# Local x transposed by DMA with its sums later in the block, and quarter products issued one by one

## The chip, the cores and the metric

The kernel runs on one core of one Trainium2 chip. A core has a matrix engine (TensorE, PE in the profile, with its weight loads PEld), VectorE (DVE), ScalarE (ACT), GpSimd (POOL) and SyncE (SP), each with its own in-order instruction queue, and 16 DMA engines that move data between memories. The metric is the device time of one execution in microseconds (us). Before the change the median of three runs is 294.25 us (293.95 to 294.44). The profile is of one execution of 294.54 us, of which the program's instructions span 292.8 us; TensorE's granted clock was 0.999 of full speed.

## The reference

Attention over 8 batches, 8 heads, 576 positions and head size 64, with two fixed masks, followed by a dense layer pair on all 4608 tokens.

```python
scores = scale * np.matmul(q, k.transpose(0, 1, 3, 2))
mask_local = (rel >= 0) & (rel < stride)                     # heads 0 to 3, stride 32
mask_strided = (rel >= 0) & (pos[None, :] % stride == pos[:, None] % stride)   # heads 4 to 7
...
scores = np.where(masks[None, :, :, :], scores, -1000000000.0)
attn = exp(scores - max) / (sum + 1e-09)
x = (attn @ v).transpose(0, 2, 1, 3).reshape(4608, 512)
h = x @ w_in                                                 # 512 -> 2048
g = h * np.tanh(log1p(exp(h)))                               # Mish
out = g @ w_out                                              # 2048 -> 512
```

## The kernel before

**Tiling.** The 4608 tokens are worked in nine blocks of 512 (block t). In block t the kernel runs three things interleaved on the same engines: the first layer of block t (class `Mlp1`), the second layer of block t-1 (class `Mlp2`), and the attention of batch t+1 (class `Attn`, blocks 1 to 6 for batches 2 to 7). Blocks 7 and 8 have no attention left. x, the attention's output, is kept transposed in `xT` (128 x 4 x ring of four batches of 576 tokens): chunks 0 and 1 hold the local heads, chunks 2 and 3 the strided ones.

**Seven products for eight.** Both layers are multiplied as 2 x 2 blocks by a scheme of seven products and extra sums. For the first layer, the sums of weights lie in `wis`, the sums of x in `xs`; they are made by `x_sum` (line 370), called x0 to x3: x0 uses strided x alone, x1, x2 and x3 use local x too. The second layer has sums `gs` of the activations (`g_sum`, line 458: n for the first, then g1, g2, g3). All these sums are `tensor_tensor` operations of DVE with two operands in SBUF.

**First layer, by quarters.** `Mlp1.step` (line 402) works quarter group g (0 to 3) of the 2048 columns in named steps, on three PSUM banks be, al and E of one of two sets. A product is four matmuls of 256 columns (`prod`, line 386). Step a: product 5 into E, its cast to s5, product 1 into al, a copy be<-al. Step b: product 6 on al, its cast to s2, product 3 on E, the sum h0 = E + s2 on DVE, product 2 on be. Step c: product 7 on al, the sum h1 = al + s5 on DVE. Step d: product 4 on al. Steps U, W and H are the Mish activations of be, al and h, on ACT. Casts go to ACT where there is attention (t + 1 < 8), else to DVE; the copy be<-al is always ACT's.

**Second layer.** `Mlp2.steps` (line 539) gives 14 half steps, here m1 to m14, of eight matmuls each, in the order of products 1, 5, 2, 6, 3, 7, 4, each in two halves. After m2, m4 and m8 ACT copies a bank out; after m10 and m12 DVE adds the output sum (`add(Dv, osb...)`, lines 520 and 523) from PSUM and one SBUF operand; after m12 and m14 SP stores 256 rows. m11 and m12 write the bank al (product 7), which m12's output sum reads and which m13 (product 4) writes next.

**Attention.** Step q n computes a group of scores on PE (`qk`, line 261; strided groups 0 to 2, local groups 3 to 5), takes exp on ACT and multiplies by the mask (`mask`, line 283) on POOL; in block 2 groups 0 to 3 are masked on DVE. Steps v take from the list `v_steps` (line 721): five strided PV groups, two strided transposes, and the local part: PV, PV, transposes, PV, PV, transposes. A PV group (`pv`, line 293) is six or seven matmuls into the banks at0 and at1 in turn, a reciprocal and a multiply on DVE. A local transpose (`xt`, line 324) is six PE transposes (line 330) into PSUM and one DVE copy to `xT` (line 334).

**What sets the order.** The program's order is written out by hand: a plan string (MAIN for t = 3 to 6, MAIN2 for t = 2, PLAIN for t = 7 and 8; lines 804 to 819) names the steps in sequence, and `run` (line 712) issues each, so every engine's queue holds its instructions in the plan's order. In a plan, x, g and n are sums on DVE, m a half step of the second layer, q a group of scores, s the copy of v, e and f loads of ACT's tables for exp and Mish, D the four DMA transposes of q and k on SP's queue, R POOL's small copies that wait for them and then its loads of later batches.

Of the kernel before, what the change touches and what calls it, by code (L numbers as in the profile page):

```python
# [45 lines left out]
def kernel(ctx, tc, q, k, v, moe_w_in, moe_w_out, out):  # L46
# [69 lines left out]
    def cast(eng, out_, in_):  # L116
        if eng is Sc:
            Sc.copy(out_, in_)  # L118
        else:
            eng.tensor_copy(out_, in_)  # L120

    def add(eng, out_, a, b, op=ALU.add):
        eng.tensor_tensor(out=out_, in0=a, in1=b, op=op)  # L123
# [114 lines left out]
    class Attn:  # L238
# [54 lines left out]
        def pv(self, kind, n0, n1, bank, eng=None):  # L293
# [27 lines left out]
                in1=rden[0:m, 0:nu].unsqueeze(2).to_broadcast([m, nu, D]), op=ALU.mult,  # L321
            )

        def xt(self, kind, hf, bank, eng):
            tr = bank[:].bitcast(BF16)
            t0 = (self.b % RING) * S
            if kind == "l":
                for w in range(NW):
                    u = 12 * hf + 2 * w
                    PE.transpose(  # L330
                        tr[:, WQ * w:WQ * w + WQ], x_l[0:WQ, u:u + 2, :].rearrange("p u d -> p (u d)"),
                        ident[0:WQ, 0:WQ],
                    )
                cast(eng, xT[:, hf, t0:t0 + S], tr[:, 0:S])
            else:
                for j in range(CS):
                    u = 16 * hf + 2 * j
                    PE.transpose(  # L338
                        tr[:, PN * j:PN * j + PN], x_s[0:PN, u:u + 2, :].rearrange("p u d -> p (u d)"),
                        ident[0:PN, 0:PN],  # L340
                    )
                cast(
                    eng, xT[:, 2 + hf, t0:t0 + S].rearrange("p (n j) -> p n j", j=CS),
                    tr[:, 0:576].rearrange("p (j n) -> p n j", j=CS),
                )
# [35 lines left out]
    class Mlp1:  # L381
# [18 lines left out]
                    )  # L400

        def step(self, s, g):
            z = (self.t + g + 1) % 2
            be, al, E = [x[:] for x in SETS[z]]
            if self.eng is Dv:
                z = ((self.t + 1) % 2, 2, self.t % 2, (self.t + 1) % 2)[g]
                be, al, E = [x[:] for x in ((A1, A0, SETS[(self.t + 1) % 2][2]) if g == 1 else SETS[z])]
            h = hh[z]
            o = gT[:, 4 * g:4 * g + 4, :]
            two = lambda x: x.rearrange("p (u n) -> p u n", u=2)  # L410
            if s == "a":
                self.prod(5, g, E, True)
                cast(self.eng, s5[z][:], E)
                self.prod(1, g, al, True)
                Sc.copy(be, al)  # L415
            elif s == "b":
                self.prod(6, g, al, False)
                cast(self.eng, s2[z][:], al)
                self.prod(3, g, E, False)
                add(Dv, h[:, 0, :], E, s2[z][:])  # L420
                self.prod(2, g, be, False)
            elif s == "c":
                self.prod(7, g, al, False)
                add(Dv, h[:, 1, :], al, s5[z][:])
            elif s == "d":
                self.prod(4, g, al, False)
            elif s == "H":
                Sc.activation(  # L428
                    o[:, :, 256:512], h[:].rearrange("p i (u n) -> p (i u) n", u=2), AF.Mish
                )  # L430
            elif s == "U":
                Sc.activation(o[:, 0:2, 0:256], two(be), AF.Mish)
            elif s == "W":
                Sc.activation(o[:, 2:4, 0:256], two(al), AF.Mish)  # L434
# [130 lines left out]
    with tc.manual_schedule():  # L565
# [146 lines left out]
        def run(plan, t):  # L712
# [8 lines left out]
            def v_steps():  # L721
# [4 lines left out]
                def xt(kind, hf):  # L726
                    at.xt(kind, hf, (A0, A1)[bank[0]], Sc if t == 1 and kind == "l" else Dv)
                    bank[0] = (bank[0] + bank[1]) % 2
                P = lambda kd, r: (lambda: pv(kd, r))
                X = lambda kd, hf: (lambda: xt(kd, hf))  # L730
                if t == 1:
# [3 lines left out]
                    )  # L735
                return (
                    [P("s", r) for r in PV_S] + [X("s", 0), X("s", 1)]
                    + [P("l", r) for r in PV_L[:2]] + [X("l", 0)]
                    + [P("l", r) for r in PV_L[2:]] + [X("l", 1)]
                )  # L740
            vs_ = late + (v_steps() if at else [])
            late.clear()
            JOBS = [("s", 0), ("s", 1), ("s", 2), ("l", 0), ("l", 1), ("l", 2)]
            for w in plan.split():
                c, n = w[0], int(w[1:]) if len(w) > 1 else 0
                if c in "abcdHUW":
                    m1.step(c, n)
                elif c == "p":
                    plain(t, n, deal1[n], act=False)
# [52 lines left out]

        late = []
        MAIN = (
            "x0 m m e m m x1 s x2 g1 g2 q0 q1 m m m m g3 q2 q3 m m q4 q5 m D v m f R a0 v v m m v v b0 a1 x3 c0 v "
            "U0 v b1 d0 U1 W0 c1 v a2 d1 W1 v H0 a3 v v b2 v H1 c2 b3 c3 d2 W2 v H3 d3 n U2 U3 W3 H2"
        )
        SECOND = (
            "t0 p0 q2 p1 t1 t2 t3 w1 p2 q3 w2 p3 q5 q4 p4 h p5 p6 f v y0 D y1 p7 s v p8 R y3 y6 v y2 v p9 v v y5 y4 "
            "p10 p11 y9 p12 y8 y7 y11 v v p13 v y13 p14 y10 p15 y14 n v y12 w3 y15"  # L810
        )
        MAIN2 = (
            "v m m v m e v x0 x1 m x2 g1 q1 q0 g2 m m m m g3 q2 s q3 m m q4 q5 m D f v m v a0 R v m m v v b0 a1 x3 "
            "c0 v v b1 d0 U0 U1 W0 c1 v a2 d1 W1 v H0 a3 v v b2 v c2 H1 b3 c3 d2 W2 v H3 d3 U2 U3 W3 H2 n"
        )
        PLAIN = (
            "m m x0 g1 x1 m m x2 x3 a0 m m g2 m b0 m m m g3 m m c0 U0 a1 H0 m m b1 d0 W0 a2 c1 a3 b2 b3 c3 d1 U2 H1 "
            "W1 U1 c2 d3 W3 U3 d2 H2 W2 H3 n"
        )

        for t in range(1, NBLK):
# [40 lines left out]
```

## Time and profile before

| | us |
|---|---|
| median of three runs (lowest, highest) | 294.25 (293.95, 294.44) |
| the profiled execution | 294.54 |
| its span | 292.8 |
| a block with attention (3 to 6) | 29.59 to 29.68 |
| a plain block | 25.19 to 25.39 |

The profile page lists busy time by engine; a view by windows gives the same for stretches of the span, and the timeline lists instructions in order of time with start, duration, engine, line, operation, output<-inputs, shapes and, in brackets, how long the engine was idle before it and who ended the wait. Durations of pipelined matmuls and activations overlap, so work is read from start to start. POOL's six masks of a block (three of 72 partitions, then three of 128) run back to back; block 4's first five:

| mask | start us | us |
|---|---|---|
| strided 0 | 143.86 | 1.81 |
| strided 1 | 145.64 | 2.79 |
| strided 2 | 148.40 | 1.26 |
| local 0 | 149.63 | 2.00 |
| local 1 | 151.59 | 1.99 |

### The profile page before, as it was taken

Reading aid. Unit: us, or ns where it says so; the run is one execution under the profiler, and the core shown is the slowest. Engines: PE = TensorE matmul, PEld = TensorE weight load, DVE = VectorE, ACT = ScalarE, POOL = GpSimd, SP = SyncE. Lnnn points to the kernel's source line nnn. Section 1 sums busy time; section 2 is a strip of 40 time slices with the busy share of each in tenths; the row PEclk is TensorE's granted clock in tenths of the full one; section 3 lists DMA queues with packets and bytes.
Section 4 is the critical chain, followed back from the end, with each engine's and each line's share of the span. In section 5 each row is a group of like instructions: output and inputs, shape, how many; then the busy total and the mean of one; then the engine's idle time right before and its main releaser. Section 6 shows DMA issues by size and latency. Waiting matters only on the chain.

```text
span 292.8 us, 7799 instructions
## 1 busy us (share of the span) xinstructions
PE 282.4 (96%) x3256; PEld 223.8 (76%) x3268; DVE 205.7 (70%) x387; ACT 204.7 (70%) x361; POOL 102.7 (35%) x109
## 2 busy tenths in 40 slices
PE   8889999999999999999999999999999999999995
PEld 3564545545788888888888888888898888888884
DVE  2583548587798896688768866886688667757842
ACT  2578793769667789778977898789878526825650
POOL 8754330131614533981399039502920000000000
PEclk9999999999999999999999999999999999999999
DMA  7999999999999999999699989950110003003004
GB/s 136 179 204 202 203 194 185 174 169 150 137 154 181 204 174 70 165 223 166 32 167 215 167 39 147 231 36 2 72 73 2 2 29 118 1 3 143 2 0 143
DMA packets 94415, 35.84 MB, mean 122 GB/s; under 512 B 75804, under 2 KB 90124, under 8 KB 94380
## 3 DMA queue, kind: packets, MB, share of 16 engines
q0 software_dynamic: 61712, 18.71, 70.1%
q1 hardware_dynamic: 31708, 15.73, 24.4%
q10 hardware_dynamic: 960, 0.91, 1.0%
q8 instruction: 25, 0.41, 0.6%
q14 instruction: 10, 0.08, 0.1%
HBM read 37.87 MB, written 9.44 MB: 162 GB/s over the span
## 4 chain that ended last, share of the span: by engine, by line
PE 77%; ACT 8%; DVE 7%; issue 3%; DMA 3%; POOL 1%; ACTq 0%; POOLq 0%
PE al L129 34%; PE ee L129 19%; PE be L129 12%; PE at L129 5%; DVE hh L123 4%; PE at L310 3%; ACT s L118 3%; DMA vraw<-in_v_dram 3%; ACT gT L428 1%; PE at L338 1%; ACT Pl L281 1%; ACT gT L434 1%; DVE x_l L319 1%; ACT be L415 1%; PE at L330 1%
## 5 line engine op out<-in xcount | busy, mean ns | idle before, releaser
L129 PEld LDWEIGHTS <-w_in 128*128 128x128 bf16 x464 | 44.3, 98 | 20.6 <-issue 5.0
L129 PEld LDWEIGHTS <-gs 128*128 128x128 bf16 x512 | 48.7, 98 | 6.3 <-DVE gs L123 0.3
L129 PEld LDWEIGHTS <-wis 128*128 128x128 bf16 x472 | 44.5, 99 | 9.2 <-issue 3.2
L129 PEld LDWEIGHTS <-gT 128*128 128x128 bf16 x448 | 42.0, 98 | 10.0
L287 POOL TENSOR_TENSOR Ps<-Ps,consts_sb 72x864 bf16<-72x864 bf16 (+1 forms) x12 | 23.2, 1957 | 48.2 <-ACT Ps L281 48.2
L123 DVE TENSOR_TENSOR gs<-gT,gs 128x2048 bf16<-128x2048 bf16 x16 | 21.0, 1312 | 15.4 <-PE al L129 9.7
L129 PE MATMUL al<-wos,gs 128*128 128x256 bf16 x256 | 31.8, 273 | 0.0
L129 PE MATMUL al<-xs,wis 128*128 128x256 bf16 x208 | 30.4, 272 | 0.1
L428 ACT ACTIVATE gT<-hh 128x1024 bf16<-128x1024 f32 x26 | 27.7, 1067 | 0.0
L129 PE MATMUL al<-xT,w_in 128*128 128x256 bf16 (+1 forms) x141 | 25.8, 300 | 1.6 <-ACT gT L434 0.9
L129 PE MATMUL be<-xT,w_in 128*128 128x256 bf16 (+1 forms) x139 | 25.1, 299 | 0.2 <-issue 0.2
L287 POOL TENSOR_TENSOR Pl<-Pl,consts_sb 128x960 bf16<-128x960 bf16 (+1 forms) x14 | 22.2, 1608 | 7.6 <-ACT Pl L281 7.6
L129 PE MATMUL be<-w_out,gT 128*128 128x256 bf16 (+1 forms) x157 | 23.3, 293 | 0.2
L314 DVE RECIPROCAL rden<-at 96x6 f32<-96x6 f32 (+2 forms) x64 | 12.1, 189 | 14.6 <-PE at L310 10.8
L434 ACT ACTIVATE gT<-al 128x512 bf16<-128x512 f32 x26 | 15.6, 601 | 7.8 <-PE al L129 7.8
L319 DVE TENSOR_TENSOR x_s<-at,rden 72x448 bf16<-72x448 f32 (+1 forms) x34 | 19.9, 585 | 1.2
L123 DVE TENSOR_TENSOR hh<-al,s 128x512 f32<-128x512 f32 x26 | 17.8, 684 | 2.8 <-PE al L129 2.4
L123 DVE TENSOR_TENSOR hh<-ee,s 128x512 f32<-128x512 f32 x26 | 17.8, 684 | 2.5 <-ACT s L118 1.9
L123 DVE TENSOR_TENSOR gs<-gT 128x2048 bf16<-128x2048 bf16 x16 | 19.5, 1218 | 0.0
L129 PE MATMUL al<-w_out,gT 128*128 128x256 bf16 (+1 forms) x143 | 19.3, 284 | 0.1
L120 DVE COPY xT<-at 128x576 bf16<-128x576 bf16 x25 | 14.5, 597 | 4.5 <-PE at L330 4.3
L319 DVE TENSOR_TENSOR x_l<-at,rden 96x384 bf16<-96x384 f32 x30 | 16.6, 553 | 1.0
(185 smaller groups left out, 573.9 us busy)
## 6 DMA issues: line engine op xcount, KB each, us to landing
out_dram<-osb SPq DMA_DIRECT2D x16, 512.0 KB, 3.4
vraw<-in_v_dram POOLq DMA_DIRECT2D x8, 288.0 KB, 6.1
w_out<-in_moe_w_out_dram POOLq DMA_DIRECT2D x4, 512.0 KB, 15.4
ql<-in_q_dram POOLq DMA_DIRECT2D x7, 288.0 KB, 10.8
vl<-in_v_dram POOLq DMA_DIRECT2D x7, 288.0 KB, 9.1
kl<-in_k_dram POOLq DMA_DIRECT2D x5, 384.0 KB, 11.0
ks<-in_k_dram POOLq DMA_DIRECT2D x6, 288.0 KB, 8.2
qs<-in_q_dram POOLq DMA_DIRECT2D x6, 288.0 KB, 9.1
```

Of the source, the lines that this page charges most:

```text
L118: Sc.copy(out_, in_)
L120: eng.tensor_copy(out_, in_)
L123: eng.tensor_tensor(out=out_, in0=a, in1=b, op=op)
L129: PE.matmul(o, lhsT=lhsT, rhs=rhs, start=start, stop=stop, skip_group_check=True)
L281: Sc.activation(pt[0:n, e, 0:o], ps[e][0:n, 0:o], AF.Exp, scale=scale)
L287: meng.tensor_tensor(out=pm, in0=pm, in1=mk[0:n, :].unsqueeze(1).unsqueeze(1).to_broadcast([n, 2, nu, w]), op=ALU.mult,)
L310: PE.matmul(po[:, n - n0, :], lhsT=pt[0:r, c0:c0 + 128], rhs=rhs, start=True, stop=True)
L314: Dv.reciprocal(rden[0:m, 0:nu], po[0:m, :, D])
L319: Dv.tensor_tensor(out=x[0:m, n0:n1, :], in0=po[0:m, :, 0:D], in1=rden[0:m, 0:nu].unsqueeze(2).to_broadcast([m, nu, D]), op=ALU.mult,)
L330: PE.transpose(tr[:, WQ * w:WQ * w + WQ], x_l[0:WQ, u:u + 2, :].rearrange("p u d -> p (u d)"), ident[0:WQ, 0:WQ],)
L428: Sc.activation(o[:, :, 256:512], h[:].rearrange("p i (u n) -> p (i u) n", u=2), AF.Mish)
L434: Sc.activation(o[:, 2:4, 0:256], two(al), AF.Mish)
```

## The change

The local part of `v_steps` no longer transposes on TensorE: `last_l` runs the second PV group of a half and then `xt_by_dma`, which issues one DMA transpose of 96 partitions x 768 elements from `x_l` to `xT` on SP's queue. This holds for t = 2 to 6, batches 3 to 7. Steps a and b are cut: a keeps product 5 and its cast, i has product 1 and the copy, b product 6 and its cast, j product 3 and the sum h0, k product 2. A and B are a and b with the cast on the other engine. The plans are rewritten with the new steps; in MAIN and MAIN2 the sums x0, x1 and x2 stand behind most of the second layer's half steps instead of among the first ones. The first block's plan (SECOND) stays.

```diff
--- before.py
+++ after.py
@@ -321,6 +321,13 @@
                 in1=rden[0:m, 0:nu].unsqueeze(2).to_broadcast([m, nu, D]), op=ALU.mult,
             )
 
+        def xt_by_dma(self, hf):
+            t0 = (self.b % RING) * S
+            nc.sync.dma_start_transpose(
+                xT[:, hf, t0:t0 + S].rearrange("c (w n) -> c w n", w=NW),
+                x_l[0:WQ, 12 * hf:12 * hf + 12, :].rearrange("p u d -> p (u d)"),
+            )
+
         def xt(self, kind, hf, bank, eng):
             tr = bank[:].bitcast(BF16)
             t0 = (self.b % RING) * S
@@ -400,6 +407,9 @@
                     )
 
         def step(self, s, g):
+            eng = self.eng
+            if s in "AB":
+                s, eng = s.lower(), Dv if eng is Sc else Sc
             z = (self.t + g + 1) % 2
             be, al, E = [x[:] for x in SETS[z]]
             if self.eng is Dv:
@@ -410,14 +420,17 @@
             two = lambda x: x.rearrange("p (u n) -> p u n", u=2)
             if s == "a":
                 self.prod(5, g, E, True)
-                cast(self.eng, s5[z][:], E)
+                cast(eng, s5[z][:], E)
+            elif s == "i":
                 self.prod(1, g, al, True)
                 Sc.copy(be, al)
             elif s == "b":
                 self.prod(6, g, al, False)
-                cast(self.eng, s2[z][:], al)
+                cast(eng, s2[z][:], al)
+            elif s == "j":
                 self.prod(3, g, E, False)
                 add(Dv, h[:, 0, :], E, s2[z][:])
+            elif s == "k":
                 self.prod(2, g, be, False)
             elif s == "c":
                 self.prod(7, g, al, False)
@@ -726,6 +739,10 @@
                 def xt(kind, hf):
                     at.xt(kind, hf, (A0, A1)[bank[0]], Sc if t == 1 and kind == "l" else Dv)
                     bank[0] = (bank[0] + bank[1]) % 2
+
+                def last_l(hf):
+                    pv("l", PV_L[2 * hf + 1])
+                    at.xt_by_dma(hf)
                 P = lambda kd, r: (lambda: pv(kd, r))
                 X = lambda kd, hf: (lambda: xt(kd, hf))
                 if t == 1:
@@ -735,15 +752,14 @@
                     )
                 return (
                     [P("s", r) for r in PV_S] + [X("s", 0), X("s", 1)]
-                    + [P("l", r) for r in PV_L[:2]] + [X("l", 0)]
-                    + [P("l", r) for r in PV_L[2:]] + [X("l", 1)]
+                    + [w for hf in range(2) for w in (P("l", PV_L[2 * hf]), lambda hf=hf: last_l(hf))]
                 )
             vs_ = late + (v_steps() if at else [])
             late.clear()
             JOBS = [("s", 0), ("s", 1), ("s", 2), ("l", 0), ("l", 1), ("l", 2)]
             for w in plan.split():
                 c, n = w[0], int(w[1:]) if len(w) > 1 else 0
-                if c in "abcdHUW":
+                if c in "ABabcdijkHUW":
                     m1.step(c, n)
                 elif c == "p":
                     plain(t, n, deal1[n], act=False)
@@ -802,20 +818,22 @@
 
         late = []
         MAIN = (
-            "x0 m m e m m x1 s x2 g1 g2 q0 q1 m m m m g3 q2 q3 m m q4 q5 m D v m f R a0 v v m m v v b0 a1 x3 c0 v "
-            "U0 v b1 d0 U1 W0 c1 v a2 d1 W1 v H0 a3 v v b2 v H1 c2 b3 c3 d2 W2 v H3 d3 n U2 U3 W3 H2"
+            "m m g1 g2 m e m q0 q1 m s m m m q2 q3 g3 m m q4 q5 D m f x0 x1 v R x2 m v a0 v i0 m v m v b0 v a1 i1 j0 "
+            "k0 x3 c0 v b1 j1 d0 U0 c1 k1 W0 A2 U1 i2 v d1 v W1 H0 A3 i3 v v b2 j2 b3 k2 H1 c2 c3 k3 d2 n W2 H2 j3 U3 "
+            "U2 d3 H3 W3"
         )
         SECOND = (
             "t0 p0 q2 p1 t1 t2 t3 w1 p2 q3 w2 p3 q5 q4 p4 h p5 p6 f v y0 D y1 p7 s v p8 R y3 y6 v y2 v p9 v v y5 y4 "
             "p10 p11 y9 p12 y8 y7 y11 v v p13 v y13 p14 y10 p15 y14 n v y12 w3 y15"
         )
         MAIN2 = (
-            "v m m v m e v x0 x1 m x2 g1 q1 q0 g2 m m m m g3 q2 s q3 m m q4 q5 m D f v m v a0 R v m m v v b0 a1 x3 "
-            "c0 v v b1 d0 U0 U1 W0 c1 v a2 d1 W1 v H0 a3 v v b2 v c2 H1 b3 c3 d2 W2 v H3 d3 U2 U3 W3 H2 n"
+            "v m m v m e v g1 m q1 g2 q0 s m m m m g3 x0 x1 q3 m q2 x2 m q5 q4 m v D f m v A0 v i0 m R v m v B0 x3 k0 "
+            "A1 i1 c0 v j0 v b1 j1 k1 d0 U0 W0 U1 c1 v a2 i2 d1 v W1 H0 A3 v i3 v b2 j2 k2 H1 c2 b3 j3 k3 c3 d2 d3 W2 "
+            "H3 U2 U3 H2 W3 n"
         )
         PLAIN = (
-            "m m x0 g1 x1 m m x2 x3 a0 m m g2 m b0 m m m g3 m m c0 U0 a1 H0 m m b1 d0 W0 a2 c1 a3 b2 b3 c3 d1 U2 H1 "
-            "W1 U1 c2 d3 W3 U3 d2 H2 W2 H3 n"
+            "x0 m g1 m m g2 x1 m x2 a0 x3 m i0 m m B0 j0 m m g3 c0 m m m k0 A1 i1 m b1 U0 m d0 W0 j1 H0 a2 i2 c1 k1 "
+            "A3 i3 b2 j2 B3 j3 k3 c3 H1 k2 U1 c2 d1 U2 d3 W1 W3 n d2 H2 H3 W2 U3"
         )
 
         for t in range(1, NBLK):
```

## Prediction

> **What bounds the kernel now.** I read the page first, then busy time by block, then the timelines of one block. All durations are of the one profiled execution: span 292.8 us, 294.54 us with what lies around it; the median of the runs shown is 294.25. I add my sum to 294.25.
>
> ```profile
> span 292.8 us, 7799 instructions
> PE 282.4 (96%) x3256; PEld 223.8 (76%) x3268; DVE 205.7 (70%) x387; ACT 204.7 (70%) x361; POOL 102.7 (35%) x109
> ```
> ```profile
> 77.61:107.33 29.72, 29.35 (x377) 25.52 (x375) 26.27 (x53) 21.22 (x39) 10.92 (x14) 1.00 1.90 176
> 136.92:166.52 29.60, 29.24 (x365) 25.61 (x364) 22.59 (x43) 24.41 (x44) 17.47 (x16) 1.00 1.26 146
> 251.19:276.38 25.19, 24.86 (x224) 21.88 (x224) 17.85 (x27) 12.94 (x22) 0.00 (x0) 1.00 0.12 43
> ```
> The columns are length, then busy us of PE, PEld, DVE, ACT, POOL. PE issues nearly without pause: blocks 3 to 6 (plan MAIN) take 29.60 each, the plain blocks 7 and 8 take 25.2, block 2 (MAIN2) takes 30.3 between its first second-layer matmul (77.45) and the next block's (107.76). So an edit is worth what it changes in PE's issue time and in PE's few waits. The PE timeline of block 4 shows both:
>
> ```profile
> 160.10 0.60 PE L129 MATMUL ee<-xs,wis 128*128 128x256 bf16 x4
> 160.89 0.60 PE L129 MATMUL al<-xT,w_in 128*128 128x256 bf16 x4 [0.19 <-ACT gT L434]
> 161.32 0.42 PE L330 MATMUL at<-consts_sb,x_l 96*128 96x96 bf16 x6
> 161.58 0.35 PE L310 MATMUL at<-vl,Pl 128*128 128x65 bf16 x6
> ...
> 165.93 0.42 PE L330 MATMUL at<-consts_sb,x_l 96*128 96x96 bf16 x6
> 166.52 0.60 PE L129 MATMUL al<-xs,w_in 128*128 128x256 bf16 x4 [0.17 <-DVE hh L123]
> ```
> Read start to start. A product of four matmuls costs 0.44, six transposes cost 161.58 - 161.32 = 0.26. Two waits remain: 160.89 - (160.10 + 0.44) = 0.35 for an activation W, and 166.52 - (165.93 + 0.26) = 0.33 for a sum on DVE. Without these waits and without its 12 local transposes a MAIN block is 29.60 - 0.68 - 0.52 = 28.40 of PE issue.
>
> **What looks like a gain.** 60 transposes go (12 in each of blocks 2 to 6): 60 x 0.043 = 2.6 us of PE. Ten DVE copies of 0.46 go with them; DVE is off the path there, so nothing is counted. In their place stand ten DMA transposes on SP's queue, each half the size of qTl's, which lands thus:
>
> ```profile
> DMA to landing us min/median/max: 3.7/4.2/7.2
> ```
> They are issued behind the block's four q/k transposes and two stores, which SP finishes 16 to 17 us into the block, and at about 24 and 26 us; the first reader is sum x1, 11 us into the next block, or 5 us into plain block 7, so they have some 14 and 7.6 us and cost nothing. A landing later than that would hold DVE at x1 and the products behind it. POOL's hold copies and loads keep their place behind the masks.
>
> Then the order. I walked PE, ACT and DVE through one block of the new order, with a product at 0.44, a half step m of the second layer at 0.875, 0.2 from a PE end to its reader, 0.06 back, DVE casts and adds starting 0.60 apart, ACT copies and Mish 0.49 (wide Mish 0.95). The same rules give the two waits of before. The end of a new MAIN block keeps 0.24 of the wait for W1 (the activation takes 0.86 from the last product to PE, 0.62 of PE work lies between) and 0.06 at 4(2), since the sums now come early enough; the cast moved to DVE by A2 and A3 finds DVE free. So far 28.40 + 0.30, about 28.85 with small waits: 0.75 less per block. Block 2 has less: its last sum h1 takes 0.94 from product 7(3) to 4(3), and with the transposes gone only one product of 0.44 covers it, so 0.5 is waited; 30.3 becomes 29.85. A plain block comes to 24.95 from 25.2: its products close up, but the next m1 waits about 0.37 for W3, whose activation queues behind W1. Sum if nothing else changed: 4 x 0.75 + 0.45 + 2 x 0.25 = 3.95 less, 290.3.
>
> **What speaks against it: the sums move under the masks.** In blocks 3 to 6 POOL masks the scores, six instructions back to back for 10.6 us. Before, x0 to x2 ran in the first 4 us of a block, ahead of them. Now they stand behind m10's output sum on DVE, in the middle of them. What a DVE sum of two SBUF operands does there is shown by the one such sum of before that meets a mask, g3 (DVE, then POOL):
>
> ```profile
> 138.30 0.42 DVE L123 TENSOR_TENSOR xs<-xT 128x512 bf16<-128x512 bf16 x1
> 138.75 0.42 DVE L123 TENSOR_TENSOR xs<-xT,xs 128x512 bf16<-128x512 bf16 x1
> 140.65 1.22 DVE L123 TENSOR_TENSOR gs<-gT,gs 128x2048 bf16<-128x2048 bf16 x1
> ...
> 149.92 0.69 DVE L123 TENSOR_TENSOR osb<-al,o 128x512 f32<-128x512 f32 x1
> ```
> ```profile
> 145.15 1.60 DVE L123 TENSOR_TENSOR gs<-gT,gs 128x2048 bf16<-128x2048 bf16 x1 [2.14 <-PE al L129]
> ```
> ```profile
> 143.86 1.81 POOL L287 TENSOR_TENSOR Ps<-Ps,consts_sb 72x864 bf16<-72x864 bf16 x1 [11.37 <-ACT Ps L281]
> 145.64 2.79 POOL L287 TENSOR_TENSOR Ps<-Ps,consts_sb 72x864 bf16<-72x864 bf16 x1
> 148.40 1.26 POOL L287 TENSOR_TENSOR Ps<-Ps,consts_sb 72x576 bf16<-72x576 bf16 x1
> 149.63 2.00 POOL L287 TENSOR_TENSOR Pl<-Pl,consts_sb 128x960 bf16<-128x960 bf16 x1
> ```
> The first mask is undisturbed (1.81). g3 is issued while it runs, takes 1.60 instead of 1.22, and ends 1.08 after the mask. The second mask, of the same shape, takes 2.79 and ends 1.68 after g3. That is no shared slowing: each waits until the other's whole instruction is over. The same three numbers (1.54 to 1.61, 1.81, 2.79) stand in all four blocks. The output sum at 149.92, which reads PSUM and one SBUF operand, keeps its 0.69 under a mask.
>
> Now the new block, in us from its first m. PE: m8 ends at 7.59, m10 at 9.88, m12 at 12.34, and m13 is due at 13.64. The exps of q0 start at 5.59 (ACT's seven instructions from W2 to the copy be<-al end at 3.8; table load, copy o5 follow), so the masks start at 6.69. Mask 0 ends 8.50; g3 ends 9.58; mask 1 ends 11.26. x0, issued at 10.68 behind the output sum, ends 11.26 + 0.28 = 11.54 (g3's 1.08 is 0.14 under its 1.22; 0.42 - 0.14). Mask 2 was waiting and takes its turn, to 12.69. x1 needs x0's result, so it comes after mask 2 and ends 12.97; the first local mask follows, to 14.84. The reciprocal and multiply of the first PV fit behind x1 (to 13.83); x2, issued at 13.75, waits for that mask and ends 15.12. Queued behind x2 on DVE is m12's output sum: 15.05 to 15.74. m13 overwrites the bank which that sum reads, so PE stands there: 15.79 instead of 13.64. The third PV waits too (its bank is freed by the first multiply), but m13's wait contains that. From there the walk runs on 2.15 later and DVE catches up within 3 us. A MAIN block is 28.40 + 0.30 + 2.15 = 30.85, that is 1.25 more than before; four of them 5.0.
>
> In block 2 the score masks and the first local one are on DVE and only two local masks on POOL. There x2 waits for one of them (0.7 late); the first PV's multiply and through its bank the third PV follow, 0.75 on PE; later casts on DVE (A0, B0, A1) add 0.2. 29.85 + 0.95 gives 0.3 to 0.5 over before; I take 0.3. The bounds are -0.45 (x2 first) and +2.2 (x2 behind both POOL masks, 0.9 and 2.0 long).
>
> Sum: 5.0 + 0.3 - 0.5 (plain blocks) = 4.8 more: 297.6 of span, **299.0** us of run.
>
> No row of before shows an x sum against a mask; its nearest is g3, same operation, type and operands in SBUF, which I take. The bounds are none (-3.95 in all) and, if the late PVs also push later ones, 0.7 more a block.
>
> The Trainium skill, page "SBUF — State Buffer", section "Who interferes with whom", says that a VectorE tensor_tensor with both inputs in SBUF contends with a GpSimd instruction that reads SBUF, that whichever was issued first holds the shared ports for its whole instruction, and that with one SBUF input it does not. The four g3 rows agree, and by that rule the x sums behave as I took them and the sum is the same 299.0; it leaves less chance to the next two rivals.
>
> **Rivals.** (1) The x sums pass the masks freely. Place: x0 to x2 in blocks 3 to 6; it decides if m12's output sum ends before 13.6. For it: they are a quarter of g3's size. Against: g3's rows. Then the walk without the lock holds: 294.25 - 3.95 = 290.3, faster. Chance 0.11. (2) x1 slips in between x0 and mask 2. x2 then meets mask 2's end only, m12's sum ends at 14.1, but the second PV waits for mask 2 (13.15); PE loses about 0.7: a MAIN block is 29.45, total -0.6 + 0.3 - 0.5, 293.4. Against: mask 2 has waited since 11.26 when x0 ends, and x1 has not been issued. Chance 0.09. (3) It stacks: block 2 at +2.2 and 0.5 more in each MAIN block: 299.0 + 1.9 + 2.0 = 302.9. For it: block 2's DVE is busy 26.27 of 29.72 and gets four more casts. Chance 0.10. (4) The DMA transposes land late, say 10 us: only x1 in block 7 waits, 2.4, giving 301.4. Chance 0.03.
>
> **Numbers.** Forecast 299.0 with 0.66 (its own range 296.5 to 301.5), the rest as above. Range 293.0 to 302.5: it takes in rival 2 and leaves out rival 1 and about half of 3, under 0.2. Below 0.2% (0.6 us) this kernel's runs, 293.95 to 294.44, tell nothing. Faster: rival 1 and most of 2, 0.16; same 0.06; slower 0.78.
>
> **What would show it.** In blocks 3 to 6 of the changed profile: x0, x1, x2 recorded at 0.7 to 1.5 instead of 0.42, mask 2 and the first local mask unchanged to 0.4 longer; m12's output sum starting over 15 us into the block; a PE wait of about 2 us before m13 with DVE named; blocks of 30.8. Plain blocks at 24.9 to 25.0, no wait for the DMA at x1. Wrong if the x rows stay at 0.42 under the masks or if m13 follows its predecessor at once.

## The result and the profile after

The changed kernel takes 321.2 us (median of four runs, 320.37 to 322.28) against 294.35 for the kernel before in the same runs: a ratio of 1.0917, with a 95% interval of 1.0872 to 1.0961. The forecast was 299.0, in a range of 293.0 to 302.5. The first lines of the page of after, its row of TensorE's granted clock, and its windows by block (columns as before: length, then PE, PEld, DVE, ACT, POOL, the clock, DMA share, GB/s):

```profile
span 318.6 us, 7696 instructions
...
PE 290.5 (91%) x3196; PEld 226.8 (71%) x3208; DVE 228.7 (72%) x381; ACT 204.0 (64%) x357; POOL 105.4 (33%) x109
...
PEclk9999999999999997799969997799969999999999
```
```profile
77.16:107.00 29.84, 29.50 (x369) 25.35 (x368) 28.44 (x56) 19.72 (x36) 11.67 (x14) 1.00 1.64 173
107.00:143.84 36.84, 31.91 (x356) 26.80 (x354) 28.59 (x42) 23.85 (x42) 17.66 (x16) 0.91 1.95 149
143.84:179.38 35.54, 30.74 (x354) 26.02 (x353) 29.14 (x43) 23.63 (x42) 17.97 (x16) 0.90 1.11 136
...
277.86:302.79 24.93, 24.70 (x224) 21.90 (x224) 15.58 (x23) 15.02 (x26) 0.00 (x0) 1.00 0.12 44
```
Measured from first m to first m, the blocks stand thus (all blocks in this text are measured so):

| block | before us | after us | forecast us |
|---|---|---|---|
| 2 | 30.31 | 29.99 | 30.6 |
| 3 to 6 | 29.59, 29.59, 29.68, 29.81 | 36.68, 35.54, 36.50, 37.21 | 30.85 each |
| 7, 8 | 25.19, 25.19 | 24.94, 24.94 | 24.95 |

The whole loss lies in the four MAIN blocks: they are 27.3 us longer together, and everything else is a little shorter. In them the clock is 0.90 to 0.91 where it was 1.00, and PE is idle for 4.8 to 5.2 us of each (length less busy time). The timeline of block 4, whose first m starts at 143.67, shows where: first DVE, then POOL's six masks, then PE.

```profile
151.52 1.71 DVE L123 TENSOR_TENSOR gs<-gT,gs 128x2048 bf16<-128x2048 bf16 x1 [1.55 <-ACT Ps L281]
153.82 0.69 DVE L123 TENSOR_TENSOR osb<-ee,o 128x512 f32<-128x512 f32 x1 [0.59 <-PE ee L129]
154.43 5.90 DVE L123 TENSOR_TENSOR xs<-xT 128x512 bf16<-128x512 bf16 x1
160.36 1.02 DVE L123 TENSOR_TENSOR xs<-xT,xs 128x512 bf16<-128x512 bf16 x1
```
```profile
150.33 1.81 POOL L287 TENSOR_TENSOR Ps<-Ps,consts_sb 72x864 bf16<-72x864 bf16 x1 [14.77 <-ACT Ps L281]
152.11 2.79 POOL L287 TENSOR_TENSOR Ps<-Ps,consts_sb 72x864 bf16<-72x864 bf16 x1
154.87 1.27 POOL L287 TENSOR_TENSOR Ps<-Ps,consts_sb 72x576 bf16<-72x576 bf16 x1
156.11 1.98 POOL L287 TENSOR_TENSOR Pl<-Pl,consts_sb 128x960 bf16<-128x960 bf16 x1
158.06 1.98 POOL L287 TENSOR_TENSOR Pl<-Pl,consts_sb 128x960 bf16<-128x960 bf16 x1
160.01 1.08 POOL L287 TENSOR_TENSOR Pl<-Pl,consts_sb 128x384 bf16<-128x384 bf16 x1
```
```profile
156.03 0.40 PE L310 MATMUL at<-vs,Ps 72*128 72x65 bf16 x7
160.39 1.04 PE L129 MATMUL ee<-xs,wis 128*128 128x256 bf16 x4 [3.96 <-DVE xs L123]
162.20 0.55 PE L310 MATMUL at<-vs,Ps 72*128 72x65 bf16 x7 [0.78 <-DVE x_s L319]
162.56 1.04 PE L129 MATMUL al<-xT,w_in 128*128 128x256 bf16 x4
```
x0 (the row at 154.43) is issued 10.76 into the block (10.68 in the forecast), but takes 5.90 us where the forecast had 0.86. The masks behind it do not slow: mask 2 and the first two local ones take 1.27, 1.98 and 1.98, as before the change (1.26, 2.00, 1.99). x0 gets its turn just ahead of the last local mask: it ends at 160.33, 0.3 after the fifth mask (160.04). PE has nothing but product 5(0), product 5 of quarter 0, which needs x0, and stands 3.96 us. A wait for x0 stands once in each of the four blocks, 14.1 us in all:

```profile
PE ee L129 <- DVE xs L123: 14.1, 4, 4.0
```
In blocks 4 to 6 it is 3.96 long. In block 3, where PE had already stood 1.46 us before a product of scores, it is shorter:

```profile
123.57 0.61 PE L129 MATMUL ee<-xs,wis 128*128 128x256 bf16 x4 [2.20 <-DVE xs L123]
```
The products behind the wait of block 4 also take longer, 1.04 for four matmuls where 0.60 is usual. Windows of one microsecond in the same stretch show why (the clock stands third from the end):

```profile
157.00:158.00 1.00, 0.00 (x0) 0.00 (x0) 1.00 (x1) 0.00 (x0) 1.00 (x1) 1.00 1.49 146
158.00:159.00 1.00, 0.00 (x0) 0.00 (x0) 1.00 (x1) 0.00 (x0) 1.00 (x2) 0.63 0.40 24
159.00:160.00 1.00, 0.00 (x0) 0.00 (x0) 1.00 (x1) 0.00 (x0) 1.00 (x1) 0.50 1.27 285
...
164.00:165.00 1.00, 1.00 (x7) 0.72 (x5) 0.62 (x1) 0.71 (x2) 1.00 (x2) 0.50 0.76 79
165.00:166.00 1.00, 1.00 (x16) 0.87 (x15) 0.46 (x2) 0.00 (x0) 1.00 (x3) 0.96 0.75 122
```
In block 4 TensorE's clock falls to half about 2 us into the idle time and comes back some 4.6 us after work has started again. By the trace's record of the clock it falls 2.8, 1.8, 3.8 and 4.9 us after the idle time of blocks 3 to 6 began, and stays at half for 6.8 us each time; the four falls lie 34.1, 37.5 and 37.5 us apart. The Trainium skill, page "TensorE: Matmul & The Clock Gate", Part 1, has both steps: a busy array runs at full clock, one idle window of about 3.4 us halves it, and about as much busy time releases it; the window runs freely. The trace agrees in the two levels and in the free window: the falls lie 10, 11 and 11 times 3.41 us apart. It does not agree that a whole window must be idle: the clock fell 1.8 us into the wait of block 4, and in block 3 after a wait of 2.20. How much of a window must be idle is not shown.

The DMA transposes of local x land after

```profile
DMA to landing us min/median/max: 2.5/4.8/13.4
```
and x1 waits for none of them here.

### The profile page after: what moved, and what is told of

Read it like the earlier page. It is cut to its first block, busy times and chain, and to the rows that moved or that the text cites. A ratio compares the mean times of both kernels' runs of the same rounds, so it can differ in the third digit from the quotient of the medians.

```text
span 318.6 us, 7696 instructions
## 1 busy us (share of the span) xinstructions
PE 290.5 (91%) x3196; PEld 226.8 (71%) x3208; DVE 228.7 (72%) x381; ACT 204.0 (64%) x357; POOL 105.4 (33%) x109
## 4 chain that ended last, share of the span: by engine, by line
PE 78%; DVE 11%; issue 3%; ACT 3%; DMA 2%; POOL 2%; DVEq 0%; ACTq 0%; POOLq 0%
PE al L129 37%; PE ee L129 19%; PE be L129 12%; DVE xs L123 7%; PE at L129 4%; PE at L310 4%; DMA vl<-in_v_dram 2%; DVE x_s L319 2%; ACT gT L447 1%; PE at L345 1%; ACT Pl L281 1%; PE at L337 0%; POOL qs L137 0%; DVE rden L314 0%; DVE hh L123 0%
## 5 line engine op out<-in xcount | busy, mean ns | idle before, releaser
L129 PEld LDWEIGHTS <-gs 128*128 128x128 bf16 x512 | 51.6, 103 | 8.5
L129 PE MATMUL ee<-xs,wis 128*128 128x256 bf16 x112 | 17.7, 283 | 14.1 <-DVE xs L123 14.1
L129 PE MATMUL al<-xT,w_in 128*128 128x256 bf16 (+1 forms) x141 | 27.6, 316 | 0.9 <-ACT Pl L281 0.2
L123 DVE TENSOR_TENSOR xs<-xT 128x512 bf16<-128x512 bf16 x14 | 27.6, 1970 | 0.0
L441 ACT ACTIVATE gT<-hh 128x1024 bf16<-128x1024 f32 x26 | 27.3, 1057 | 0.0
L287 POOL TENSOR_TENSOR Pl<-Pl,consts_sb 128x960 bf16<-128x960 bf16 (+1 forms) x14 | 23.4, 1693 | 5.3 <-ACT Pl L281 5.3
L426 ACT COPY be<-al 128x512 f32<-128x512 f32 x26 | 15.1, 580 | 13.0 <-PE al L129 13.0
L129 PE MATMUL al<-w_out,gs 128*128 128x256 bf16 x128 | 22.4, 335 | 0.0
L118 ACT COPY s<-al 128x512 f32<-128x512 f32 x23 | 13.5, 587 | 13.5 <-PE al L129 13.3
L310 PEld LDWEIGHTS <-Ps 72*128 72x128 bf16 x256 | 14.2, 106 | 8.7 <-issue 5.5
```

The costliest lines, as they stand in the source:

```text
L129: PE.matmul(o, lhsT=lhsT, rhs=rhs, start=start, stop=stop, skip_group_check=True)
L287: meng.tensor_tensor(out=pm, in0=pm, in1=mk[0:n, :].unsqueeze(1).unsqueeze(1).to_broadcast([n, 2, nu, w]), op=ALU.mult,)
L310: PE.matmul(po[:, n - n0, :], lhsT=pt[0:r, c0:c0 + 128], rhs=rhs, start=True, stop=True)
L441: Sc.activation(o[:, :, 256:512], h[:].rearrange("p i (u n) -> p (i u) n", u=2), AF.Mish)
```

## The experiments

Three things could lie behind the extra 22 us: the late sums under the masks, the DMA transposes, and the new order of the products. All ratios are to the kernel before, run beside each version. Lines left out of an edit are marked "...".

**1. Sums early.** The changed kernel with x0 to x2 back at the start of MAIN.

```diff
-"m m g1 g2 m e m q0 q1 ... q4 q5 D m f x0 x1 v R x2 m v a0 ...
+"m m x0 x1 x2 g1 g2 m e m q0 q1 ... q4 q5 D m f v R m v a0 ...
```


> The changed kernel with x0, x1 and x2 of blocks 3 to 6 put back behind the block's second half step, ahead of POOL's masks; all else as changed. Theory (the sums wait under the masks, and the half clock that follows PE's idle time is their consequence): x rows at 0.42 again, granted clock 1.00, MAIN blocks of 28.8 to 29.0, some 290 us of run. Rival (the DMA transposes, or the finer order, cost the time): MAIN blocks stay at 35 to 37, 315 us or more.

Measured: 313.81, ratio 1.0674 (1.0613 to 1.0736); blocks 3 to 6 of 37.29, 37.05, 34.08 and 28.88. The expected 290 is missed, and the rival's 315 almost met. The sums take 0.42 (one x1 1.54) and PE no longer waits for x0, but another wait has come. DVE in block 4:

```profile
150.33 0.42 DVE L123 TENSOR_TENSOR xs<-xT,xs 128x512 bf16<-128x512 bf16 x1 [4.21 <-DMA xT<-x_l]
...
152.15 2.84 DVE L123 TENSOR_TENSOR gs<-gT 128x2048 bf16<-128x2048 bf16 x1
154.91 7.44 DVE L120 COPY vs<-vraw 72x2048 bf16<-72x2048 bf16 x1
```
x1 needs the DMA transposes, which land up to 12.0 us after their issue, so DVE stands (7.9 us at most), and what is queued behind x1, g2 and the copies of v, is pushed under the masks: the copy of v takes 7.44 there. Block 6 is the one block ahead of which POOL has issued no loads of q and k, and it takes 28.88, as the walk without the lock had it (28.85). So there are two causes, and early sums trade the first for the second.

**2. Late sums alone.** The kernel before, local transposes on TensorE, with x0 and x1 moved behind m11 and x2 one PV later. (In the changed kernel they stand behind m11 too.)

```diff
-"x0 m m e m m x1 s x2 g1 g2 q0 q1 ... q4 q5 m D v m f R ...
+"m m e m m s g1 g2 q0 q1 ... q4 q5 m x0 x1 D v x2 m f R ...
```


> The kernel before with x0 and x1 moved behind the eleventh half step and x2 one PV later, as the change has them; PE transposes and the old order of products stay. Theory: x0 at 5 to 6 us in blocks 3 to 6, PE idle about 4 us there, clock 0.90 in these blocks, 315 to 322 us. Rival (it takes the DMA transposes or the finer order): 294 to 297 us.

Measured: 325.88 in one run, blocks of 37.44 to 37.75, 7.9 more than before each. In block 4 x0 takes

```profile
155.70 5.74 DVE L123 TENSOR_TENSOR xs<-xT 128x512 bf16<-128x512 bf16 x1
```
The late sums alone, with no DMA transpose and no new order, make more than the whole loss.

**3. Work in the wait.** The changed kernel with 18 matmuls whose result nobody reads, ahead of product 5(0), so that TensorE stays busy while x0 waits.

```diff
+elif c == "z":
+    unread(n, SETS[(t + 1) % 2][2])
-"... x0 x1 v R x2 m v a0 ...
+"... x0 x1 v R x2 m v z18 a0 ...
```


> The changed kernel with 18 matmuls that nothing reads (3.9 us at full clock) between the second PV and product 5 of quarter 0 in blocks 3 to 6, where PE waits for x0. Theory (about 2 us of each block is PE work at half clock after that idle time): the clock stays at 1.00, and with more work the kernel is faster, about 313 us. Rival (DVE's late sums alone set the time): 321 us; if the added work is on the path, 336 us.

Measured: 313.09, ratio 1.0633 (1.0606 to 1.0660): 8 us faster than the changed kernel for 72 more matmuls in all. The clock is 1.00 throughout, blocks 3 to 6 take 34.33 to 34.67 where they took 35.54 to 37.21. Half clock cost 2.0 us a block. PE in block 4:

```profile
154.51 4.05 PE L129 MATMUL ee<-wis 128*128 128x512 bf16 x18
158.63 0.60 PE L129 MATMUL ee<-xs,wis 128*128 128x256 bf16 x4
160.45 0.37 PE L310 MATMUL at<-vs,Ps 72*128 72x65 bf16 x7 [1.22 <-DVE x_s L319]
```
The second PV starts at 154.27 and costs 0.21, so at full clock product 5(0) is 4.15 late (158.63 - 154.27 - 0.21), and the third PV another 1.38 (160.45 - 158.63 - 0.44): 5.5 us of waiting a block, which is what these blocks have over 28.9.

**4. DMA transposes alone.** The kernel before, early sums and old order, with its two local transposes of a block issued as DMA transposes.

```diff
-[P("l", r) for r in PV_L[:2]] + [X("l", 0)]
+[P("l", r) for r in PV_L[:2]] + [lambda: at.xt_by_dma(0)]
...
```


> The kernel before with the local transposes of batches 3 to 7 by DMA in place of PE transposes and DVE copies, old order and old places of the sums. Theory: 2.6 us of PE work go, but the second six of each block covered a wait for DVE's last sum that now grows by 0.26, so 1.3 to 2.0 less: 292.4 to 293. Rival (x1, early in the next block, waits for the landing and delays the sums g1 behind it): 295 us or more.

Measured: 320.06, ratio 1.0857 (1.0837 to 1.0878); blocks of 39.02, 38.07, 37.91 and 29.81. x1 waits for the landing three times, up to 7.6 us, and what follows runs into the masks. Block 6 again is not slower. By itself this part too loses some 25 us.

**5. Sums right behind g3.** The changed kernel with "g3 x0 x1 x2" in MAIN, so that DVE has the sums ready as soon as g3 has had the ports.

> The changed kernel with x0, x1, x2 right behind g3 on DVE, so that DVE has two-SBUF sums back to back when g3 wins the ports after the first mask. Theory: an engine that has its next instruction ready keeps the ports. Then x0, x1 and x2 take 0.42 each behind g3, mask 1 takes over 3.5 us instead of 2.79, products 5 wait for nothing, TensorE's clock stays at 1.00, blocks 3 to 6 take 29 to 30.5 and the span is 290 to 296. Rival: POOL takes the ports after g3 whatever waits; then x0 takes 5 us or more as in the changed kernel and m10's and m12's output sums queue behind it, blocks of 36 and a span of 318 or more.

Measured: 324.64 in one run, blocks of 36.47 to 37.63. The theory, that whoever has its next instruction ready keeps the ports, falls for DVE:

```profile
153.01 1.70 DVE L123 TENSOR_TENSOR gs<-gT,gs 128x2048 bf16<-128x2048 bf16 x1 [1.55 <-ACT Ps L281]
154.62 7.17 DVE L123 TENSOR_TENSOR xs<-xT 128x512 bf16<-128x512 bf16 x1
```
x0 now waits through mask 1 as well and again ends just behind the fifth mask (161.79, as that mask ends at 161.52).

**6. No masks on POOL.** The changed kernel with the masks of blocks 3 to 6 on DVE.

```diff
-at.mask(*JOBS[n], Dv if t == 1 or t == 2 and n in (0, 1, 2, 3) else Po)
+at.mask(*JOBS[n], Dv if t != 2 or n in (0, 1, 2, 3) else Po)
```


> The changed kernel with all masks of blocks 3 to 6 on DVE instead of POOL, the sums late and the transposes by DMA as changed. Nothing is left on POOL that reads SBUF but its small copies, so x0, x1 and x2 take 0.42 each. If the lock under the masks is what loses, the blocks come to 29 to 31 (DVE has some 6 us more work per block and stands in its own order) and the span to 291 to 298. If the late sums lose for another reason, such as their place in DVE's queue, the blocks stay at 35 or more.

Measured: 297.36 in one run, span 295.6, blocks of 30.69 to 30.90, clock 1.00. The sums stand as late as in the changed kernel and behind more work, and take 0.42:

```profile
144.77 0.60 DVE L287 TENSOR_TENSOR Ps<-Ps,consts_sb 72x864 bf16<-72x864 bf16 x1 [0.23 <-ACT Ps L281]
...
150.47 0.42 DVE L123 TENSOR_TENSOR xs<-xT 128x512 bf16<-128x512 bf16 x1
```
Without POOL beside them the late sums, with the masks' own work on DVE, cost some 2 us a block over 28.7 (0.81 and 0.61 of it are waits of PE for x0 and for the third PV's bank) instead of 7.8.

**7. Both causes out, badly.** Sums early and the local transposes on TensorE again, but put where the changed kernel issues its DMA: right behind the PV they read.

```diff
-at.xt_by_dma(hf)
+xt("l", hf)
```


> The changed kernel with both of its suspected costs taken out: the sums x0, x1, x2 back at the start of blocks 3 to 6, ahead of the masks, and the local x transposed on TensorE again, so that only the finer order of the products is left. If the late sums and the late landing of the DMA transposes are the whole loss, nothing waits in blocks 3 to 6: each is the 28.88 us measured for block 6 with early sums plus 12 transposes at 0.043, so 29.4 against 29.6 to 29.8 before; with plain blocks at 24.95 the time is 292 to 293.5. The rival, that the finer order itself loses (more moves between DVE and ACT, more waits), gives 296 or more, with waits of PE for casts in the second half of the block.

Measured: 304.04, ratio 1.0315 (1.0275 to 1.0355), blocks of 31.37 to 31.59. The x sums take 0.42 and no landing is waited for, but the transposes wait for the PV's multiply:

```profile
PE at L337 <- DVE x_l L319: 8.6, 19, 0.7
```
The miss is the experiment's own: with nothing between a PV and its transposes, PE stands four times a block there, 1.7 us in all (0.26, 0.39, 0.69 and 0.39 in block 4). Number 13 mends it.

**8. Loads behind x1.** Sums early, local x by DMA; the q and k loads that R issued in the middle of a block are issued in the next one, behind a POOL copy that reads x1's result.

```diff
-if b + 2 < B:
+if t == 1:
     load_qk(b + 2)
+elif c == "Q":
+    ...
+    Po.tensor_copy(y[:], xs[0:32, 1, 0, 0:1])
+    load_qk(b + 1)
-"m m x0 x1 x2 g1 g2 ...
+"m m x0 x1 x2 Q g1 g2 ...
```


> The sums early as in the first experiment, the local x transposed by DMA, and the q and k loads of the next batch but one, which were issued in the middle of a block, now issued on POOL behind a copy that reads x1's result, so only once the DMA transposes have landed. Theory: the DMA transposes were late (7.9 us of wait at x1) because the loads issued 6 to 8 us ahead of them filled the same DMA engines; then they land in about 4 us, x1 takes 0.42 and waits for nothing, blocks 3 to 6 come to 28.9 and the time to 290 to 291, faster than before. Rival A: the DMA transposes are slow in themselves or behind the stores and the q/k transposes; then x1 still waits several us and the time stays above 305. Rival B: the loads, now later, make the q/k transposes late; then the first products of scores in a block wait for qTs or kTl and the blocks take over 30.

Measured: 310.54, ratio 1.0522 (1.0472 to 1.0571), blocks of 38.28, 28.96, 39.72 and 28.90. The landing has come down to 2.5/2.7/6.5 (min, median, max), as the theory said, and two blocks reach 28.9. In the other two x1 still waited 1.2 and 2.4, for transposes issued 2 to 4 us behind v's loads, which had not been moved, and the copies of v behind it slid under POOL's loads and masks:

```profile
114.13 9.88 DVE L120 COPY vl<-vl 32x1280 bf16<-32x1280 bf16 x1
```
This copy, 0.48 when alone, waited through the load POOL was issuing and five masks; it ends 0.35 after the fifth (123.66). So the wait is not a matter of sums: a bf16 copy from SBUF to SBUF meets it too.

**9. Loads behind the landing.** As 8, but POOL's copy reads the last DMA transpose's result itself, and the copies of v stand behind x0.

```diff
+    t0 = (t % RING) * S
+    Po.tensor_copy(y[:], xT[0:32, 1, t0:t0 + 1])
-"m m x0 x1 x2 Q g1 g2 m e m q0 q1 m s m ...
+"Q m m x0 s x1 x2 g1 g2 m e m q0 q1 m m ...
```


> Sums early, local x by DMA, and POOL issues the q and k loads of the next batch but one only behind a copy that reads the last DMA transpose's result, at the start of the next block; the copies of v on DVE stand right behind x0, ahead of the masks. Theory: the DMA transposes land in about 4 us when no q/k loads are ahead of them, x1 waits for nothing or below 1 us, the v copies no longer stand under the masks (there one took 9.88 us in the run before), and blocks 3 to 6 are 28.9 to 29.5 each: 290 to 293. Rival: the v loads alone still delay the transposes; then x1 waits 2 us or more, POOL's loads and masks come as much later, and blocks of over 30 remain.

Measured: 289.75 in the profiled execution and 295.94, 298.15 and 299.21 in three others. Landing and block 4 of the profiled one:

```profile
DMA to landing us min/median/max: 2.6/3.4/4.6
```
```profile
136.10:164.76 28.66, 28.59 (x355) 24.99 (x353) 23.18 (x43) 23.64 (x42) 17.48 (x17) 1.00 1.29 158
```
With the q and k loads out of the way all DMA transposes of this execution land within 4.6 us instead of 12.0 or 13.4, and all four blocks take 28.65 to 28.89. That is the change's full gain, seen once. With numbers 1 and 8 it shows the second cause: the loads ahead of the transposes. v's loads still stand ahead; behind them alone landings of up to 6.5 (number 8) and 7.1 (number 10) were measured. The other three executions, which have no profile, lose to the kernel before.

**10. Slack for the landing.** As 9, with x1 and x2 behind g1 and g2 ("Q m m x0 s g1 g2 x1 x2 m e ...").

> The run with the loads behind the landing gave 289.75 once and 294 to 299 in its other three, so some of its waits must be on an edge. Here x1 and x2 stand behind g1 and g2, still ahead of the masks, so the DMA transposes have 4 us more to land. Theory: in the long executions x1 waited for a late landing and pushed the v copies and g1 under the masks; then with this slack all executions come to 289.5 to 291.5. Rival: the late part is POOL's own (loads issued late, masks late, PVs late), which this leaves as it is; then the executions still spread from 290 to 299.

Measured: 300.70 (297.04 to 307.59). The theory falls. In the profiled execution x1 waited for no landing (7.1 us at most); the copy of v did wait, for its own load, and x2 met the masks:

```profile
142.03 0.48 DVE L120 COPY vl<-vl 32x1280 bf16<-32x1280 bf16 x1 [2.59 <-DMA vl<-in_v_dram]
...
146.79 8.95 DVE L123 TENSOR_TENSOR xs<-xT 128x512 bf16<-128x512 bf16 x1
```
The likely chain, not tested: loads moved later make the next q/k transposes late, these hold up R on POOL (2.73 us for kTl in block 3), and R issues the loads of v. Whether this is also what happened in the three long executions of number 9 was not seen, since they have no profile.

**11. POOL waits for x2.** The changed kernel with one small POOL copy behind mask 1 that reads x2's result, so that masks 2 to 5 can't stand ready; x2 directly behind x1.

```diff
-at.mask(*JOBS[n], Dv if t == 1 or t == 2 and n in (0, 1, 2, 3) else Po)
+if t < 3 or n < 2:
+    at.mask(*JOBS[n], Dv if t == 1 or t == 2 and n in (0, 1, 2, 3) else Po)
+elif c == "Z":
+    ...
+    Po.tensor_copy(y[:], xs[0:32, 2, 0, 0:1])
+    for n in range(2, 6):
+        at.mask(*JOBS[n], Po)
-"... D m f x0 x1 v R x2 m v a0 ...
+"... D m f x0 x1 x2 Z v R m v a0 ...
```


> The changed kernel, with a single edit on POOL: behind mask 1 stands a small copy that reads x2's result, so masks 2 to 5 can't be started before the three sums are done, and x2 stands right behind x1. DMA transposes, late sums and all orders else as changed. Theory: what held x0 for 5.8 us was POOL's run of masks that stood ready behind each other; with the run cut x0 waits for the rest of mask 1 only (0.7 to 1.0 us in all), x1 and x2 take 0.42, the masks end 1 to 1.5 us later, nothing waits 3 us on TensorE, the clock stays at 1.00 and blocks 3 to 6 take 28.9 to 30: 290 to 295. Rival: the sums are slow under any POOL work, or the DMA transposes are late at their place; then x0 keeps 3 us or more, or x1 waits for the landing, and the time stays above 305.

Measured: 295.67, ratio 1.0037 (1.0023 to 1.0051), blocks of 29.91 to 30.20, clock 1.00: 25.5 us faster than the changed kernel by one copy of 0.18 us on POOL and x2's place, though just above the 290 to 295 expected. DVE, then PE, in block 4:

```profile
148.03 0.69 DVE L123 TENSOR_TENSOR xs<-xT 128x512 bf16<-128x512 bf16 x1
148.76 0.43 DVE L123 TENSOR_TENSOR xs<-xT,xs 128x512 bf16<-128x512 bf16 x1
149.10 0.42 DVE L123 TENSOR_TENSOR xs<-xT 128x512 bf16<-128x512 bf16 x1
```
```profile
151.11 0.23 PE L310 MATMUL at<-vs,Ps 72*128 72x65 bf16 x2 [1.16 <-POOL Ps L287]
```
The DMA transposes, the late sums and the new order are all still in. PE's wait that is left in block 4 is 1.16 for mask 2, which now comes later.

**12. The same, one mask later.** The copy behind mask 2 (`range(3, 6)`).

> The run before this one with POOL's small copy one place later, behind mask 2 instead of mask 1. Two theories of who gets the ports. (a) DVE's waiting sum gets its turn where POOL has no more than one instruction standing ready, as g3 did ahead of mask 1 and x0 ahead of the last local mask: then x0, issued under mask 1, goes ahead of mask 2 (0.7 us) and mask 2 takes 1.6 to 1.7 instead of 1.27. (b) POOL keeps the ports as long as anything stands ready: then x0 waits for mask 2 as well and takes 1.9 to 2.1. By (a) x1 waits for mask 2 (1.0 to 1.5) and x2 ends 13.2 us into the block; TensorE's wait of 1.16 for mask 2 falls to 0.4 or less, and m13 waits up to 0.5 for m12's output sum. Blocks 3 to 6 of 28.9 to 29.6, 290 to 293. By (b) x2 ends at 13.6 to 14, blocks of 29.5 to 30.2, 293 to 295.5.

Measured: 293.92, ratio 0.9973 (0.9941 to 1.0006), blocks of 29.58 to 29.86. Block 4, DVE and then the group of all masks 2 on POOL:

```profile
148.54 0.68 DVE L123 TENSOR_TENSOR xs<-xT 128x512 bf16<-128x512 bf16 x1
149.26 1.38 DVE L123 TENSOR_TENSOR xs<-xT,xs 128x512 bf16<-128x512 bf16 x1
```
```profile
L287 POOL TENSOR_TENSOR Ps<-Ps,consts_sb 72x576 bf16<-72x576 bf16 x4 | 5.8, 1455 | 0.0
```
In these rows rule (a) was right and (b) wrong: x0 goes ahead of mask 2, which takes 1.46 instead of 1.27, x1 waits for mask 2 (1.38), and x2 ends 13.18 into the block. The price of (a) was too low: three of the four blocks and the time lie above its ranges, and in those of (b), since PE waits 0.71 for the multiply behind x2.

**13. The order alone.** Sums early in MAIN, local transposes on TensorE in steps of their own, for which MAIN and MAIN2 get two more v.

```diff
-[w for hf in range(2) for w in (P("l", PV_L[2 * hf]), lambda hf=hf: last_l(hf))]
+[P("l", r) for r in PV_L[:2]] + [X("l", 0)] + [P("l", r) for r in PV_L[2:]] + [X("l", 1)]
-"m m g1 g2 m e m q0 q1 ... q4 q5 D m f x0 x1 v R x2 m v a0 ...
+"m m x0 x1 x2 g1 g2 m e m q0 q1 ... q4 q5 D m f v R m v a0 ...
-"... A3 i3 v v b2 j2 b3 k2 H1 ...
+"... A3 i3 v v b2 v j2 b3 k2 v H1 ...
```


> Sums early and the local x transposed on TensorE as before, now in steps of their own with other products between a PV and its transposes (the earlier run had put them right behind the PV, and TensorE waited there twice 0.7 to 0.8 us a block). What is left of the change is the finer order. If it loses nothing by itself, blocks 3 to 6 are 28.9 plus 12 transposes at 0.043, 29.3 to 29.6; block 2, where the sums stay late, is 30.5 to 31; plain blocks 24.95: 292.5 to 294.5. If the order itself costs, the blocks stay at 30 or more with waits for s or hh casts.

Measured: 293.20, ratio 0.9953 (0.9936 to 0.9970), blocks of 29.26 to 29.49. The finer order gains by itself, 0.32 to 0.41 a block. Block 2 took 32.25, more than expected.

**14. Block 2 too.** As 13, with block 2's sums early ("e v x0 x1 m x2 g1 q1 g2 ...").

> The run with the order alone (293.20), with the sums of block 2 early too, behind the first PVs as before the change. In that run block 2 still took 32.25, with 1.02 of TensorE's wait on the multiply that stood behind x2 on DVE. Without it block 2 comes to 30.4 to 31.2 and the whole to 291 to 292.4, faster than both kernels by 0.6% or more. Rival: the late sums of block 2 only fill DVE's idle time, and what costs there is DVE's own work (masks, casts, the copies of the transposes); then block 2 stays at 31.8 or more and the time at 292.8 to 293.6.

Measured: 293.63, ratio 0.9972 (0.9956 to 0.9987). Block 2 fell to 31.17 in the profile, but the time did not follow: numbers 13 and 14 can't be told apart by these runs. Both are 0.3% to 0.5% under the kernel before, and hold their time but for one execution of number 14 (302.34). Neither uses a DMA transpose for local x.

## Why the prediction was wrong

**The direction and the place were right.** The late sums under POOL's masks lose, with DVE named, in blocks 3 to 6 (numbers 2, 6 and 11). The parts off that path were right in size: plain blocks 24.94 (24.95), and the MAIN block without a lock 28.65 to 28.89 (28.85), shown by block 6 of number 1 and by number 9. In block 2 the bound "x2 first" came true: 29.99, with no sum held (the forecast had 30.6, the bound 29.85).

**The step that failed: "x0, issued at 10.68 behind the output sum, ends 11.26 + 0.28 = 11.54".** In block 4 x0 was issued at 10.76, mask 1 ended at 11.23 (154.90), and x0 ended at 16.66 (160.33). From g3's rows the forecast took that the one who waits comes next. What those rows showed was only that each waits for a whole instruction of the other. A mask stands ready once POOL's queue has passed its wait, and the trace has these times for block 4: mask 1 at 151.05, mask 2 at 152.68, the local ones at 153.60, 155.20 and 155.65. When mask 0 ended (152.14), only mask 1 stood ready, and g3 went ahead of it. When mask 1 ended, mask 2 and the first local one stood ready, and x0 was left out; so again after mask 2 and the first local one. After the second local mask one mask was left, and x0 went. That rule, that DVE gets in where POOL has no more than one mask standing ready, foretold number 12 and fits x0 in blocks 5 and 6 and in blocks 4 to 6 of numbers 2, 3 and 5. POOL's small copy behind the last mask, whose wait was passed at 155.75, must not count for it to fit. It does not hold everywhere: in block 5 of number 1 a copy of v, issued at 191.00, went ahead of the first local mask when mask 2 ended (193.88), and g3 ahead of the second when the first ended (196.09), though three masks stood ready at the first time and two at the second (waits passed at 191.75, 193.36 and 193.80). So what decides the turn stays open. What is shown is the run of masks: x0 took 5.76 to 5.90 in all four blocks, 5.68 to 5.74 in number 2, and 0.62 to 0.69 where the run was cut (numbers 11 and 12).

The Trainium skill, page "SBUF — State Buffer", section "Who interferes with whom", says that issue order decides who blocks. The prediction leaned on it for one mask. Here x0 was issued 1.7 us before the first local mask began, and 0.8 us before the second had passed its wait, and went behind both; the measurement decides, and the rule as stated does not hold between a waiting DVE instruction and masks of POOL that are queued ready.

**What the wrong step cost.** The forecast had PE wait 2.15 at m13. The runs have it wait at product 5(0), which stands ahead of m13, and at the third PV: 4.15 and 1.38, 5.5 together at full clock (number 3). That is 3.4 more a block, 13.5 in four.

**The term that was left out: half clock.** The forecast's longest stall was 2.15 us, and no term stood for the clock. Here the clock halves in the stall for x0, and that costs 2.0 a block, 8 in all (number 3). A stall of 2.15 would not have been safe either: in block 3 the clock halved after one of 2.20. 299.0 + 13.5 + 8 = 320.5, against 321.2 measured.

**The DMA transposes "cost nothing"**: right in the changed kernel, but not for the reason given. They do not all land in 4.2 to 7.2 us; they took up to 13.4, behind the loads that R has POOL issue shortly before and, in block 2, beside them. They cost nothing only because x1 is so late. With x1 early they cost 20 us and more (numbers 1 and 4), and with the q and k loads moved they land in 4.6 to 7.1 at most (numbers 8, 9 and 10). So the two parts of the change are tied: DMA transposes at this place want late sums, and late sums meet the masks.

**The rivals.** Of those named, "it stacks" gave the highest time, but its price (302.9) came from the same rule of one mask each. The rival for late landing had the size right (10 us and more) and the place wrong: the late ones were those of blocks 2 and 3 (13.4 and 7.9), and those that block 7's x1 reads landed in 2.5 to 2.6. No rival had x0 behind the whole run of masks, though the trace of before showed the six masks back to back, and that would have been the upper bound: x0 at the end of five masks.

## What to carry to other kernels

A DVE instruction that takes two operands from SBUF, or a bf16 copy within SBUF, should not stand where POOL has several masks ready: here its price was up to the rest of POOL's run, not one instruction, and one tiny POOL copy that depends on DVE's result cut that run. A stall of TensorE of 2 us or more may have to be priced with half-clock time behind it: the shortest that was followed by it here was 2.20 us (1.46 of waiting stood shortly before), and single waits of 1.2 to 1.6 us were not. A DMA whose landing is taken from another transfer's row should be priced with what is issued ahead of it at its new place.

## What the runs showed of the hardware

- A POOL mask of 72 x 864 bf16 takes 1.81 us; the same on DVE takes 0.60 (number 6). With all masks on DVE the changed kernel lost 1% to before instead of 9%.
- The copy of v's 32 x 1280 elements took 9.88 us instead of 0.48 behind POOL's load issue and masks (number 8).
- 72 matmuls more, put into TensorE's idle time, made the kernel 8 us faster (number 3).
